# One feed-forward stage, three PSUM banks: seven-product units with a bank for each sum, later w_out words, logits without the clearing flag

## The chip, the cores and the metric

The kernel runs on 1 core of one Trainium2 chip. The metric is device time in microseconds (us) of one execution. The engines are named as in the profile: PE (matrix multiplies), DVE (vector), ACT (scalar), POOL (GpSimd), SP (which issues the DMAs).

## What is computed

```python
a = x @ w_a; b = x @ w_b              # x: 2304 x 512 (output of a banded attention), w: 512 x 1536
x = (a * b) @ w_out                   # feed-forward, w_out: 1536 x 512
logits = x @ phi                      # phi: 512 x 32 (8 experts x 4 slots)
d = softmax(logits, over tokens);  slot_input = d.T @ x
slot_out[e] = relu(slot_input[e] @ w1[e]) @ w2[e]
c = softmax(logits, over slots);   out = c @ slot_out
```

All of it is float32 to the reader of the output. The attention ahead of it is not touched by the change.

## The kernel before

After the attention x lies transposed in SBUF in five blocks of tokens (blocks 0 to 3 up to 512 wide, block 4 256). The 1536 columns of w_a and w_b are taken 128 at a time: f = 0 to 11. The product g = a*b is never multiplied by w_out: phi is folded into w_out first, M = w_out·phi (one 128x32 piece for each f), so that logits += M_f·g_f. Four products f = 0 to 3 of all blocks are made during the attention; the rest is the stage of this change.

**Units.** For blocks 0 and 1 and f = 4 to 11 the two halves of x and of the weights are taken as 2x2 matrices, and `unit(u, f, ...)` (u = f-4 = 0 to 7) makes a and b of both blocks by seven products in place of eight. Each product is six 128x512 matmuls (two k halves, three passes of float32 split in two words). There are three sums in PSUM, A, B and C, each in a bank of its own, which PE fills in this order: A (1st product), B (2nd), A (3rd), C (4th), A (5th), B (6th), A (7th). ACT copies A, B and C out between products, and C begins as an ACT copy of the first A. At the end DVE works out B += c2 (L2098), c1 *= B (L2099), POOL c3 += c4 (L2100), DVE c3 *= A (L2104), then DVE transposes c1 and c3 (L1305, L1307).

**PSUM.** Eight banks: a tag `m` with two banks, `m2` with one, `n` with one (the logits L of all blocks, a quarter of the bank each), `t` with four (transposes, M steps, slots). `UNIT_TAGS` gives A, B, C of even units the tags m, m, m2 and of odd units m2, m, m, so that each unit takes over banks of the one before it: an odd unit's B gets the bank in which A of the unit before was, an even unit's B that of the B before, and an even unit's C that of the A before.

**What runs between the products.** `gap(x)` puts small PE steps between products: logits of two units at every second one (`L`, L1325), and the M steps of w_out: four transposes (`wo`, L1337, copied by ACT at L1339), phi times it (`Mp`, L1344), a fold (`M`, L1352). A list of extras with clocks decides at which gap each comes; `extra(..., (("C", f), 2), ...)` asks that a `wo` comes two gaps after its words. `behind(x)` puts conversions on the other engines behind products: for the next unit the weights' raw 64-bit words are read (ACT `ra`, `rb` L921; DVE `wa`, `wb`: low word L927, whole word L939; DVE differences L1977; casts L1983; second words `la`, `lt` on DVE and `lu`, `lb` on POOL, L1989). `more()` steps through the same for one piece of w_out: rebias (ACT L921, behind ACT's copy of the third product), words (DVE L927 + L939, then the DMAs that store them and load the next raw piece, L903), and the M steps. The engines run their queues in the order in which the program issues.

**After the units** blocks 2, 3 and 4 are done with plain products (L1239), while softmax steps and slots of the block before run between: `soft` reads the logits (DVE L1373), `slots` takes four `t` banks. In `step_L` the first matmul of a block has the flag `start`, and for blocks 2 and up an `ensure(("S", ...))` puts `soft` of the block two before it ahead of that.

Of the kernel before, what the change touches and what calls it, by code (L numbers as in the profile page):

```python
# [14 lines left out]
ALU = mybir.AluOpType  # L15
# [168 lines left out]
def kernel(  # L184
# [1028 lines left out]
    close_psum(att_psum)  # L1213
    ffn_psum = open_psum(m2=1, n=1, t=4)
    post = ctx.enter_context(tc.tile_pool(name="post", bufs=1))
# [96 lines left out]
    def step_L(f, blk, src):  # L1312

        ensure(("M", f, "c", 0))
        if blk not in L_n:
            if blk >= 2:
                ensure(("S", blk - 2, 0))
            L_t[blk] = L_bank[:, blk % 4, :]  # L1320
            L_n[blk] = 0
        assert blk != 1 or 0 in L_n
        ps = L_t[blk]
        for j in range(len(TILES[blk])):
            nc.tensor.matmul(  # L1325
                ps[32 * j:32 * j + 32, :], lhsT=M[:, f, :], rhs=src[:, 128 * j:128 * j + 128],
                start=(L_n[blk] == 0 and blk != 1), stop=(L_n[blk] == NF - 1), skip_group_check=True,
            )
        L_n[blk] += 1
# [26 lines left out]
    def fin_steps(blk):  # L1356
# [80 lines left out]
        def slots(b):  # L1437


            def go():  # L1440
                if b == 0:
                    st["sl"] = [bank(PS["t"], "t", [128, UNIT], f"sl{blk}_{a}") for a in range(4)]
                for j in range(nj):
# [474 lines left out]
    def m_conv(f):  # L1918
# [11 lines left out]
        def fold():  # L1930
            tr, mm, fold = m_steps(f, box)
            x = M_ORDER.index(f)
            pair = M_ORDER[x - x % 2:x - x % 2 + 2]
            last = M_ORDER[x - 2:x - 1] if x > 1 else ()
            extra(0, ("M", f, "a"), [(("M", y, "b", 0), 0) for y in last] + [(("C", f), 2)], [(tr, 0, 0)])
            at["C", f] = clock[0]
            extra(0, ("M", f, "b"), [(("M", y, "a", 0), 1) for y in pair] + [(("M", y, "c", 0), 0) for y in last], [(mm, 0, 1)])
            extra(0, ("M", f, "c"), [(("M", f, "b", 0), 1)], [(fold, 0, 0)])
# [107 lines left out]

    UNIT_TAGS = (("m", "m", "m2"), ("m2", "m", "m"))

    def unit(u, f, gap, behind):

        tags = UNIT_TAGS[u % 2]
        b = {}
        d = half_t["tmp"]

        def prod(n, x, w, first):
            if first and n not in b:
                b[n] = bank(PS[tags["ABC".index(n)]], tags["ABC".index(n)], [128, 512], f"{n}{f}")
            wm, xm = pw(f, w), XS[x]
            todo = [(wm[:, wl, 128 * k:128 * k + 128], xm[:, xl, k, :]) for k in range(2) for wl, xl in PASSES]
            for i, (lhsT, rhs) in enumerate(todo):  # L2060
                nc.tensor.matmul(b[n], lhsT=lhsT, rhs=rhs, start=first and i == 0, stop=i == 5, skip_group_check=True)  # L2061
        V = nc.vector
        prod("A", "A11", "B11", True)
        b["B"] = bank(PS[tags[1]], tags[1], [128, 512], f"B{f}")
        gap(0)
        if u:
            b["C"] = bank(PS[tags[2]], tags[2], [128, 512], f"C{f}")
            nc.scalar.copy(b["C"], b["A"])
# [34 lines left out]
        prod("A", "A22", "T4", False)  # L2103
        V.tensor_tensor(c3, c3, b["A"], ALU.mult)  # L2104
        free_half(f"w{f}_U")
        gap(3)
        behind(6)
        step_T(f, 0, c1)
# [54 lines left out]
    with tc.manual_schedule():  # L2163
# [43 lines left out]
        def run_unit(n, f):  # L2207
# [27 lines left out]
            def behind(x):  # L2235
# [34 lines left out]
                elif x == 4:  # L2270
                    do("ht", "la")
                    more()
                elif x == 5:
                    do("lt")
                    more()
            unit(u, f, gap, behind)
            for blk in range(2):
                pend.append((0, f, blk))
            if f == NF - 1:
# [5 lines left out]
                let_ring_go()  # L2285
                m_n[0] = 2
            for name in ("xt2_0", "xt2_1", "gt2", "gt3"):
# [161 lines left out]
```

## Time and profile before

| | us |
|---|---|
| median of 3 runs | 523.38 |
| the three runs | 520.12, 523.38, 523.43 |
| the profiled execution | 521.03 |
| its span, first to last instruction | 519.0 |
| PE busy | 488.6 |
| DVE busy | 333.6 |
| ACT busy | 240.3 |
| the eight units, start to end on PE | 218.97 to 317.51 |

The span is what the trace covers; the execution's own time is 2 us longer. Times inside the trace are counted from the start of the span. The units fill about a fifth of it.

### The profile page before, as it was taken

What the parts mean: (1) busy time and instruction counts of PE and PEld (TensorE: products, weight loads), DVE (VectorE), ACT (ScalarE), POOL (GpSimd) and SP (SyncE); (2) the same over time, 40 slices, a digit from 0 to 9 for tenths busy, and PEclk for the clock granted to TensorE, in tenths of its full rate; (3) what the DMA queues carried; (4) which work ended last, traced back from release to release, by engine and by line L of the source; (5) the groups of instructions that cost most, each with busy time, mean ns of one, the idle gap of its engine ahead of it and who ended that gap; (6) DMA issues with size and microseconds to landing.
All of it is one profiled execution on the core that took longest, in us unless ns stands there. A gap on an engine that the chain in (4) does not pass through costs nothing.

```text
span 519.0 us, 15098 instructions
## 1 busy us (share of the span) xinstructions
PE 488.6 (94%) x6083; PEld 383.2 (74%) x6083; DVE 333.6 (64%) x1004; ACT 240.3 (46%) x692; POOL 132.7 (26%) x204
## 2 busy tenths in 40 slices
PE   7897899899989999989999999999999999999993
PEld 6775678778768899977767677767888988943552
DVE  5878786765764379879899976555466545342132
ACT  3775748576677234555556553331222332522122
POOL 6778777554530002012232231000000000101000
PEclk9998899999999999999999999999999999999998
DMA  9999977868791045596875435598628265699996
GB/s 176 214 177 171 186 123 130 130 121 116 105 291 43 3 125 169 185 301 192 271 266 188 149 123 180 204 352 309 255 83 278 87 239 187 265 319 341 349 359 236
DMA packets 147181, 103.81 MB, mean 200 GB/s; under 512 B 98344, under 2 KB 131368, under 8 KB 145960
## 3 DMA queue, kind: packets, MB, share of 16 engines
q1 hardware_dynamic: 145000, 102.32, 70.3%
q8 instruction: 48, 0.79, 0.7%
q10 hardware_dynamic: 2112, 0.52, 0.6%
q14 instruction: 21, 0.17, 0.1%
HBM read 87.10 MB, written 15.73 MB: 198 GB/s over the span
## 4 chain that ended last, share of the span: by engine, by line
PE 49%; DVE 4%; ACT 2%; DMA 2%; issue 1%; SPq 0%; DVEq 0%; ACTq 0%
PE b L1239 10%; PE a L1239 10%; PE A L2061 7%; PE B L2061 4%; PE sl L1447 3%; PE h L1695 3%; PE L L1325 3%; PE C L2061 2%; PE so L1681 2%; DMA ex<-in_moe_w_dram 2%; PE wo L1337 1%; DVE gn L1305 1%; PE T L1298 1%; PE Mp L1344 1%; PE stp L1518 1%
## 5 line engine op out<-in xcount | busy, mean ns | idle before, releaser
L587 ACT ACTIVATE P<-P,nm 128x128 f32<-128x128 f32 x128 | 49.9, 393 | 20.5 <-DVE nm L580 20.5
L970 PE MATMUL a<-xt,h_w 128*128 128x512 f32 x144 | 40.7, 413 | 1.4 <-DVE xt L696 1.1
L580 DVE CUSTOM_DVE_ANT_0 P<-s,lmask 128x128 f32<-128x128 f32 x128 | 28.8, 285 | 19.3 <-PE s L562 19.3
L1654 POOL TENSOR_TENSOR c<-CE,c 128x128 fp32r<-128x128 f32 (+1 forms) x5 | 2.9, 575 | 148.0 <-ACT c L1653 139.9
L970 PE MATMUL b<-xt,h_w 128*128 128x512 f32 x144 | 38.8, 405 | 0.0
L482 POOL TENSOR_SCALAR vw<-vw 32x896 f32<-32x896 f32 (+1 forms) x33 | 34.3, 1039 | 14.3 <-DMA vw<-in_v_l_dram 12.3
L1989 POOL TENSOR_TENSOR h_w_U<-scratch,h_w_U 128x512 fp32r<-128x512 f32 (+1 forms) x16 | 18.6, 1179 | 51.2 <-ACT h_w_U L1983 47.6
L970 PEld LDWEIGHTS a<-xt,h_w 128*128 128x128 f32 x144 | 25.9, 192 | 6.9 <-DVE xt L696 1.5
L970 PEld LDWEIGHTS b<-xt,h_w 128*128 128x128 f32 x144 | 25.5, 188 | 5.6 <-issue 1.1
L927 DVE TENSOR_SCALAR wr<-wr 128x512 int32<-128x512 int32 x36 | 23.5, 653 | 2.8 <-DMA wr<-in_moe_w_a_dram 2.5
L587 ACT ACTIVATION_READ_ACCUMULATOR P<-P,nm 128x1 f32 x128 | 24.3, 190 | 0.0
L2151 DVE TENSOR_TENSOR h_w<-h_w 128x512 fp32r<-128x512 f32 x24 | 16.3, 678 | 12.2 <-ACT h_w L2150 12.2
L1239 PE MATMUL a<-xt3a,h_w 128*128 128x384 f32 x120 | 22.9, 338 | 0.3 <-DVE gt L1244 0.3
L1239 PE MATMUL b<-xt3a,h_w 128*128 128x384 f32 x120 | 22.9, 339 | 0.0
L637 ACT COPY PT<-tp 128x512 f32<-128x512 f32 x32 | 18.6, 584 | 8.5 <-PE tp L632 8.2
L1262 ACT COPY gT<-a 128x512 f32<-128x512 f32 (+2 forms) x12 | 5.8, 485 | 34.0 <-PE L L1325 18.6
L1239 PEld LDWEIGHTS a<-xt3a,h_w 128*128 128x128 f32 x120 | 20.8, 188 | 0.9 <-DVE gt L1244 0.5
L1239 PEld LDWEIGHTS b<-xt3a,h_w 128*128 128x128 f32 x120 | 20.8, 188 | 0.9 <-issue 0.4
L632 PE MATMUL tp<-ident,P 128*128 128x128 f32 x128 | 20.2, 281 | 0.1
L562 PE MATMUL s<-kt,qt 64*32 64x128 f32 x1024 | 20.0, 291 | 0.1
L1239 PE MATMUL b<-xt3b,h_w 128*128 128x256 f32 x144 | 19.9, 288 | 0.0
L921 ACT ACTIVATE wr<-wr 128x512 f32<-128x512 f32 x28 | 19.2, 690 | 1.2 <-DMA wr<-in_moe_w_out_dram 0.9
(328 smaller groups left out, 1209.2 us busy)
## 6 DMA issues: line engine op xcount, KB each, us to landing
ex<-in_moe_w_dram SPq DMA_DIRECT2D x62, 512.0 KB, 6.5
wr<-in_moe_w_a_dram SPq DMA_DIRECT2D x12, 512.0 KB, 5.3
wr<-in_moe_w_b_dram SPq DMA_DIRECT2D x12, 512.0 KB, 5.3
wr<-in_moe_w_out_dram SPq DMA_DIRECT2D x12, 512.0 KB, 4.1
h_w<-wd SPq DMA_DIRECT2D x24, 256.0 KB, 3.7
wd<-scratch SPq DMA_DIRECT2D x16, 256.0 KB, 5.2
out_dram<-ob SPq DMA_DIRECT2D x7, 512.0 KB, 6.6
rawk<-in_k_l_dram SPq DMA_DIRECT2D x48, 64.0 KB, 3.5
```

Of the source, the lines that this page charges most:

```text
L482: nc.gpsimd.tensor_scalar(dst, src, 1.0, 1.0, ALU.mult, ALU.mult)
L562: nc.tensor.matmul(boxes[h]["s"][32 * (w % 4):32 * (w % 4) + 32, w // 4, :], lhsT=qt[rows, 32 * w:32 * w + 32], rhs=win_keys(kt, w)[rows], ...
L580: nc.vector.tensor_tensor_reduce(P[:, t, :], s[:, t, :], lmask[:, (t + 1) // 2, :], -scale, 3.0e38, ALU.add, ALU.min, nm[:, t:t + 1])
L587: nc.scalar.activation(P[:, t, :], P[:, t, :], AF.Exp, bias=nm[:, t:t + 1], scale=-1.0, accum_out=z_t[i][:, h, t:t + 1],)
L632: nc.tensor.transpose(box["ps"][:, t, :], P[:, t, :], ident)
L637: nc.scalar.copy(PT, box["ps"])
L921: nc.scalar.activation(hf, hf, AF.Prelu, scale=REBIAS, alpha=-TO_SIGN)
L927: nc.vector.tensor_scalar(v, v, 29, None, ALU.logical_shift_right)
L970: nc.tensor.matmul(box["ps"], lhsT=lhsT, rhs=rhs, start=(k + idx == 0), stop=(k == 3 and idx == 2))
L1239: nc.tensor.matmul(ps, lhsT=lhsT, rhs=rhs, start=(idx == 0), stop=(idx == 11))
L1989: eng.tensor_tensor(t[:, 1, c:], scratch(which)[:, c:], t[:, 0, c:].bitcast(F32), ALU.subtract)
L2061: nc.tensor.matmul(b[n], lhsT=lhsT, rhs=rhs, start=first and i == 0, stop=i == 5, skip_group_check=True)
```

## The change

It edits five things, all in the stage above.

1. The pools become m 2, m2 1, n 1, t 3 and a new tag `c` 1: A always takes `m` (its two banks in turn), B always `m2`, C always `c`. The slots of a block take three `t` banks and `c`.
2. DVE's last operation of a unit, c3 *= A, is issued after `gap(3)`. The M steps `words` of w_out come behind `lt` after the sixth product's sums, where they stood ahead of B += c2, the first of the sums; the step that enters the fold comes one later.
3. `wo` asks for four gaps after the words in place of two, which moves the M steps into other gaps and other units.
4. Logits of blocks 1, 2 and 3 have no `start` flag, only blocks 0 and 4 (block 4 shares a quarter with block 0). The `ensure` of `soft` stays for block 4 alone.
5. The counter by which plain products choose `m` or `m2` starts at 0 after the units, not 2.

```diff
@@ -1211,7 +1211,7 @@
     nc.sync.dma_start(out=phi_sb, in_=phi.rearrange("(k p) s -> p k s", p=128))
     att.release()
     close_psum(att_psum)
-    ffn_psum = open_psum(m2=1, n=1, t=4)
+    ffn_psum = open_psum(m2=1, n=1, t=3, c=1)
     post = ctx.enter_context(tc.tile_pool(name="post", bufs=1))
     pages.extend((post, f"q{n}") for n in range(6))
     build_late_consts(post)
@@ -1315,8 +1315,8 @@
 
         ensure(("M", f, "c", 0))
         if blk not in L_n:
-            if blk >= 2:
-                ensure(("S", blk - 2, 0))
+            if blk == 4:
+                ensure(("S", 2, 0))
             L_t[blk] = L_bank[:, blk % 4, :]
             L_n[blk] = 0
         assert blk != 1 or 0 in L_n
@@ -1324,7 +1324,7 @@
         for j in range(len(TILES[blk])):
             nc.tensor.matmul(
                 ps[32 * j:32 * j + 32, :], lhsT=M[:, f, :], rhs=src[:, 128 * j:128 * j + 128],
-                start=(L_n[blk] == 0 and blk != 1), stop=(L_n[blk] == NF - 1), skip_group_check=True,
+                start=(L_n[blk] == 0 and blk in (0, 4)), stop=(L_n[blk] == NF - 1), skip_group_check=True,
             )
         L_n[blk] += 1
 
@@ -1439,7 +1439,7 @@
 
             def go():
                 if b == 0:
-                    st["sl"] = [bank(PS["t"], "t", [128, UNIT], f"sl{blk}_{a}") for a in range(4)]
+                    st["sl"] = [bank(PS[t], t, [128, UNIT], f"sl{blk}_{a}") for a, t in enumerate("tttc")]
                 for j in range(nj):
                     for c0, g in g_unit(blk, 4 * j + b):
                         for a in range(4):
@@ -1932,7 +1932,7 @@
             x = M_ORDER.index(f)
             pair = M_ORDER[x - x % 2:x - x % 2 + 2]
             last = M_ORDER[x - 2:x - 1] if x > 1 else ()
-            extra(0, ("M", f, "a"), [(("M", y, "b", 0), 0) for y in last] + [(("C", f), 2)], [(tr, 0, 0)])
+            extra(0, ("M", f, "a"), [(("M", y, "b", 0), 0) for y in last] + [(("C", f), 4)], [(tr, 0, 0)])
             at["C", f] = clock[0]
             extra(0, ("M", f, "b"), [(("M", y, "a", 0), 1) for y in pair] + [(("M", y, "c", 0), 0) for y in last], [(mm, 0, 1)])
             extra(0, ("M", f, "c"), [(("M", f, "b", 0), 1)], [(fold, 0, 0)])
@@ -2044,27 +2044,25 @@
             return post.tile([128, n], F32, tag="gT", bufs=2, name="gT")
         return moe_p.tile([128, n], F32, tag="a", bufs=2, name="gT_a")
 
-    UNIT_TAGS = (("m", "m", "m2"), ("m2", "m", "m"))
+    UNIT_TAGS = dict(A="m", B="m2", C="c")
 
     def unit(u, f, gap, behind):
 
-        tags = UNIT_TAGS[u % 2]
         b = {}
         d = half_t["tmp"]
 
         def prod(n, x, w, first):
             if first and n not in b:
-                b[n] = bank(PS[tags["ABC".index(n)]], tags["ABC".index(n)], [128, 512], f"{n}{f}")
+                b[n] = bank(PS[UNIT_TAGS[n]], UNIT_TAGS[n], [128, 512], f"{n}{f}")
             wm, xm = pw(f, w), XS[x]
             todo = [(wm[:, wl, 128 * k:128 * k + 128], xm[:, xl, k, :]) for k in range(2) for wl, xl in PASSES]
             for i, (lhsT, rhs) in enumerate(todo):
                 nc.tensor.matmul(b[n], lhsT=lhsT, rhs=rhs, start=first and i == 0, stop=i == 5, skip_group_check=True)
         V = nc.vector
         prod("A", "A11", "B11", True)
-        b["B"] = bank(PS[tags[1]], tags[1], [128, 512], f"B{f}")
         gap(0)
         if u:
-            b["C"] = bank(PS[tags[2]], tags[2], [128, 512], f"C{f}")
+            b["C"] = bank(PS["c"], "c", [128, 512], f"C{f}")
             nc.scalar.copy(b["C"], b["A"])
         else:
             c1 = g_t[f, 0] = g_dest(512)
@@ -2101,9 +2099,9 @@
         free_half(f"w{f}_B")
         behind(5)
         prod("A", "A22", "T4", False)
-        V.tensor_tensor(c3, c3, b["A"], ALU.mult)
         free_half(f"w{f}_U")
         gap(3)
+        V.tensor_tensor(c3, c3, b["A"], ALU.mult)
         behind(6)
         step_T(f, 0, c1)
         step_T(f, 1, c3)
@@ -2269,9 +2267,10 @@
                     do("t12", "t34", "ha")
                 elif x == 4:
                     do("ht", "la")
-                    more()
                 elif x == 5:
                     do("lt")
+                    more()
+                elif x == 6:
                     more()
             unit(u, f, gap, behind)
             for blk in range(2):
@@ -2283,7 +2282,7 @@
                 w_t[f, 0] = w_t[f, "A"]
                 held[f"w{f}_0"] = held.pop(f"w{f}_A")
                 let_ring_go()
-                m_n[0] = 2
+                m_n[0] = 0
             for name in ("xt2_0", "xt2_1", "gt2", "gt3"):
                 if name in spilled and pages and u:
                     t = restore(name, F32R if name[0] == "x" else F32)
```

On DVE this is the end of unit 3 (B7, A7 are its sums; wr2_9 and cv are w_out's words, the L1989 rows are la and lt of unit 4), before:

```order
L1989 TENSOR_TENSOR h_w4_A_3578<-scratch_3523,h_w4_A_3578 128x512
L927 TENSOR_SCALAR wr2_9_4288<-wr2_9_4288 128x512
L939 SCALAR_TENSOR_TENSOR cv_4393<-wr2_9_4288 128x512
L2098 TENSOR_TENSOR B7_4324<-B7_4324,h_tmp_3526 128x512
L2099 TENSOR_TENSOR gT_a_4371<-gT_a_4371,B7_4324 128x512
L1989 TENSOR_TENSOR h_w4_A_3578<-scratch_3523,h_w4_A_3578 128x512
L2104 TENSOR_TENSOR gT_a_4388<-gT_a_4388,A7_4317 128x512
L1305 STREAM_TRANSPOSE gn0_0_3774<-gT_a_4371 128x5x32
```

and after, where c1 *= B and lt stand ahead of the two words (L927, L939), and c3 *= A alone behind them:

```order
L1989 TENSOR_TENSOR h_w4_A_3581<-scratch_3526,h_w4_A_3581 128x512
L2096 TENSOR_TENSOR B7_4312<-B7_4312,h_tmp_3529 128x512
L2097 TENSOR_TENSOR gT_a_4368<-gT_a_4368,B7_4312 128x512
L1989 TENSOR_TENSOR h_w4_A_3581<-scratch_3526,h_w4_A_3581 128x512
L927 TENSOR_SCALAR wr2_9_4281<-wr2_9_4281 128x512
L939 SCALAR_TENSOR_TENSOR cv_4406<-wr2_9_4281 128x512
L2104 TENSOR_TENSOR gT_a_4385<-gT_a_4385,A7_4300 128x512
L1305 STREAM_TRANSPOSE gn0_0_3777<-gT_a_4368 128x5x32
```

On PE these are the last product of unit 3 and the start of unit 4 up to its C (wo9, Mp8 and Mp9 are M steps; L the logits of the two units before; gt1 block 1's g of the first four f), before:

```order
L2061 MATMUL A7_4317<-xt1_1_1762,h_w4_U_3620 128x512 x6
L2061 MATMUL A8_4423<-xt0_0_596,h_w4_A_3578 128x512 x6
L1337 MATMUL wo9_4431<-ident_82,cv_4393 128x128 x4
L2061 MATMUL B8_4430<-S1_3517,h_w4_A_3578 128x512 x6
L2061 MATMUL A8_4423<-S2_3518,h_w4_A_3578 128x512 x6
L1325 MATMUL L_3497<-gT_4261,M_3491 32x128 x4
L1325 MATMUL L_3497<-gT_4274,M_3491 32x128 x4
L1325 MATMUL L_3497<-gT_a_4371,M_3491 32x128 x4
L1325 MATMUL L_3497<-gT_a_4388,M_3491 32x128 x4
L1344 MATMUL Mp8_4481<-woT_4330,phi_sb_88 32x128 x4
L1344 MATMUL Mp9_4488<-woT_4436,phi_sb_88 32x128 x4
L1325 MATMUL L_3497<-gt1_2017,M_3491 32x128 x8
```

and after, where B8 follows A8 with nothing between, wo9 stands behind the logits, and the two Mp are gone (they come in unit 5):

```order
L2060 MATMUL A7_4300<-xt1_1_1762,h_w4_U_3623 128x512 x6
L2060 MATMUL A8_4426<-xt0_0_596,h_w4_A_3581 128x512 x6
L2060 MATMUL B8_4438<-S1_3520,h_w4_A_3581 128x512 x6
L2060 MATMUL A8_4426<-S2_3521,h_w4_A_3581 128x512 x6
L1325 MATMUL L_3500<-gT_4250,M_3494 32x128 x4
L1325 MATMUL L_3500<-gT_4263,M_3494 32x128 x4
L1325 MATMUL L_3500<-gT_a_4368,M_3494 32x128 x4
L1325 MATMUL L_3500<-gT_a_4385,M_3494 32x128 x4
L1325 MATMUL L_3500<-gt1_2017,M_3494 32x128 x8
L1337 MATMUL wo9_4485<-ident_82,cv_4406 128x128 x4
L2060 MATMUL C8_4433<-xt0_1_913,h_w4_A_3581 128x512 x6
```

On DVE this is the place behind the units where `soft` of block 0 (lt0) stands beside the transposes of block 2's g (gt2), before:

```order
L1305 STREAM_TRANSPOSE gn2_2_4926<-gt2_4812 128x5x32
L1307 STREAM_TRANSPOSE gn2_0_4924<-gt2_4812 128x32
L1373 COPY lt0_4935<-L_3497 128x128
L1375 TENSOR_REDUCE mb0_4936<-lt0_4935 128x1
L1377 TENSOR_SCALAR nm0_4937<-mb0_4936 128x1
L1305 STREAM_TRANSPOSE gn2_0_4924<-gt2_4812 128x5x32
L1305 STREAM_TRANSPOSE gn2_1_4925<-gt2_4812 128x5x32
```

and after, where it stands two pieces of gt2 later, behind the last:

```order
L1305 STREAM_TRANSPOSE gn2_1_4928<-gt2_4795 128x5x32
L1305 STREAM_TRANSPOSE gn2_2_4929<-gt2_4795 128x5x32
L1307 STREAM_TRANSPOSE gn2_0_4927<-gt2_4795 128x32
L1373 COPY lt0_4962<-L_3500 128x128
L1375 TENSOR_REDUCE mb0_4963<-lt0_4962 128x1
L1377 TENSOR_SCALAR nm0_4964<-mb0_4963 128x1
L2149 TENSOR_TENSOR h_w4_U_3623<-h_w4_U_3623 128x512
```

## Rows read from the trace of the kernel before

**Rows 1.** Stretches of the span: busy us of each engine, granted clock, DMA share, GB/s.
```profile
219.10:316.00 96.90, 92.54 (x623) 72.36 (x622) 81.70 (x179) 54.64 (x116) 26.14 (x22) 1.00 0.63 206
345.00:380.00 35.00, 35.00 (x352) 27.81 (x353) 18.61 (x54) 7.76 (x15) 0.00 (x0) 1.00 0.72 261
455.00:519.00 64.00, 55.00 (x538) 26.84 (x535) 19.44 (x47) 14.76 (x41) 2.17 (x6) 0.96 1.00 325
```
**Rows 2.** Waits of PE in 219 to 345: us in total, times, longest.
```profile
PE B L2061 <- ACT woT L1339: 2.2, 3, 0.7
PE B L2061 <- DVE gT L2104: 1.9, 2, 1.7
PE L L1325 <- DVE lt L1373: 1.0, 1, 1.0
```
**Rows 3.** Timeline of PE in the units: start, us, tile; in brackets idle before.
```profile
233.90 1.62 PE L2061 MATMUL B<-S,h_w_A 128*128 128x512 f32 x6 [1.69 <-DVE gT L2104]
...
245.67 0.60 PE L1337 MATMUL wo<-ident,cv 128*128 128x128 f32 x4
246.02 1.63 PE L2061 MATMUL B<-S,h_w_A 128*128 128x512 f32 x6
...
266.16 1.55 PE L2061 MATMUL A<-xt,h_w_U 128*128 128x512 f32 x6
267.55 0.63 PE L2061 MATMUL A<-xt,h_w_A 128*128 128x512 f32 x2
...
270.88 1.70 PE L2061 MATMUL B<-S,h_w_A 128*128 128x512 f32 x6 [0.71 <-ACT woT L1339]
...
274.17 0.64 PE L1325 MATMUL L<-gT,M 128*32 128x128 f32 x16
...
284.83 1.62 PE L2061 MATMUL B<-S,h_w_A 128*128 128x512 f32 x6 [0.74 <-ACT woT L1339]
...
293.22 1.77 PE L2061 MATMUL A<-xt,h_w_A 128*128 128x512 f32 x6
...
299.57 0.65 PE L1325 MATMUL L<-gT,M 128*32 128x128 f32 x16
```
**Rows 4.** Timeline of DVE at the end of units 3, 4 and 7.
```profile
268.26 0.41 DVE L927 TENSOR_SCALAR wr<-wr 128x512 int32<-128x512 int32 x1
268.71 0.69 DVE L939 SCALAR_TENSOR_TENSOR cv<-wr 128x512 int32<-128x512 int32 x1
...
270.04 0.69 DVE L2099 TENSOR_TENSOR gT_a<-gT_a,B 128x512 f32<-128x512 f32 x1
...
279.90 1.52 DVE L927 TENSOR_SCALAR wr<-wr 128x512 int32<-128x512 int32 x1
...
316.39 0.70 DVE L2098 TENSOR_TENSOR B<-B,h_tmp 128x512 f32<-128x512 f32 x1 [5.85 <-PE B L2061]
```
**Rows 5.** Timeline of POOL at the end of units 4 and 7.
```profile
279.80 1.34 POOL L2100 TENSOR_TENSOR gT<-gT,h_tmp 128x512 f32<-128x512 f32 x1 [4.44 <-ACT M L1353]
...
315.62 1.29 POOL L2100 TENSOR_TENSOR gT_a<-gT_a,h_tmp 128x512 f32<-128x512 f32 x1 [3.34 <-ACT gT_a L2094]
```
**Rows 6.** Units 3, 4, 5 and 6, columns as in the first group.
```profile
257.00:267.50 10.50, 10.28 (x47) 8.29 (x46) 9.62 (x24) 6.91 (x13) 4.01 (x3) 1.00 0.86 274
267.50:282.10 14.60, 13.67 (x115) 10.07 (x115) 14.17 (x32) 7.60 (x17) 3.55 (x3) 1.00 0.61 201
282.10:293.20 11.10, 10.36 (x47) 8.31 (x46) 10.74 (x26) 7.08 (x13) 3.72 (x3) 1.00 0.52 159
293.20:307.50 14.30, 13.60 (x115) 10.06 (x114) 12.31 (x26) 7.01 (x16) 3.48 (x3) 1.00 0.49 169
```
**Rows 7.** Timeline of DVE behind the units: `soft` of block 0.
```profile
322.12 0.25 DVE L1373 COPY lt<-L 128x128 f32<-128x128 f32 x1
```
**Rows 8.** Timeline of PE among block 4's transposes T.
```profile
441.40 0.60 PE L1298 MATMUL T<-ident,a_two 128*128 128x128 f32 x4
```
**Rows 9.** Timeline of ACT at the same place: copies of T.
```profile
441.38 1.20 ACT L1299 COPY h_tmp<-T 128x256 f32<-128x256 f32 x4 [2.83 <-PE T L1298]
```
**Rows 10.** Issues of w_out's raw loads in 219 to 325: count, KB, median us to landing.
```profile
wr<-in_moe_w_out_dram SPq DMA_DIRECT2D x6, 512.0 KB, 4.0
```

## The prediction

> **What bounds the kernel now.** I first read the stretches of the span. In the units PE is busy 92.54 of 96.90 us and DVE 81.70 at a granted clock of 1.00, so PE sets the end and DVE stands close behind it; the DMA share is 0.63. In 455 to 519 PE is busy 55.00 of 64.00 us and the DMA share is 1.00: there the transfers set the end [rows 1]. Then PE's waits in the units: 2.2 us in three waits of B, which the view puts down to ACT's woT, and 1.9 in two put down to DVE's c3 *= A [rows 2]. The releaser has to be checked against which bank is whose. In unit 4, B8 has the bank of B7, which is free when c1 *= B has read it. That operation runs 270.04 + 0.69 = 270.73 [rows 4], and B8 starts at 270.88 [rows 3]. ACT's woT merely ended in the same tenth: the releaser is DVE. In odd units B has the bank of the A before, and c3 *= A is two operations later on DVE. So all five waits say one thing: the next unit's B waits for DVE's last sums, and ahead of those sums stand w_out's words, 0.41 + 0.69 us in unit 3 [rows 4].
>
> How much is lost there is more than the idle time, since the first products around the wait are stretched as well. An undisturbed product takes 1.39 us from start to start (266.16 to 267.55), a `wo` 0.35 (245.67 to 246.02) [rows 3]. Unit 4 needs 274.17 - 267.55 = 6.62 us for A, wo, B and A, where 3 x 1.39 + 0.35 = 4.52 would do: 2.10 lost. Unit 6 needs 299.57 - 293.22 = 6.35: 1.83 lost. Unit 1 idles 1.69, unit 5 idles 0.74 [rows 3], and the second of the c3 waits, in unit 3, is 1.9 - 1.7 = 0.2 [rows 2]. Sum: 2.10 + 1.83 + 1.69 + 0.74 + 0.2 = **6.6 us**.
>
> **The change part by part.**
>
> *Banks and the place of the words.* With B always in its own bank, B waits for c1 *= B of the unit before in all units, never for c3 *= A, and A alternates between two banks, so c3 *= A has a whole unit's time. On DVE c1 *= B and lt now come ahead of the words, that is 1.10 us earlier (0.41 + 0.69), and 2.2 earlier where the low word takes 1.52 [rows 4]. What the next B needs: the sixth product ends 1.39 before the unit does, then B += c2 and c1 *= B at 0.7 each [rows 4] end at about the end of the unit, and lt 0.7 after it, while the next B starts 1.39 after it and reads what lt wrote from its third matmul on. So there is a margin of about 1.4 us if DVE is on time, and the 6.6 go. Where DVE is late, some of it stays.
>
> Is DVE on time? In units 3 to 6 DVE is busy 9.62 + 14.17 + 10.74 + 12.31 = 46.84 us of 50.5 [rows 6]. PE's need there is 50.5 less the losses 0.2 + 2.10 + 0.74 + 1.83 = 4.87, so 45.6. By these sums DVE would be the bound by 1.2 us. But DVE's time holds a stretch that depends on the place: the low word took 0.41 in unit 3 and 1.52 in unit 4 [rows 4], where POOL's c3 += c4 ran from 279.80 for 1.34 [rows 5]. After the change c3 += c4 starts beside B += c2 and c1 *= B, and the words come later. Beside the same addition B += c2, which reads PSUM, isn't stretched: in unit 7 it takes 0.70 at 316.39 [rows 4], with POOL busy from 315.62 for 1.29 [rows 5]. If each of the four units is rid of one such stretch of 1.1, DVE needs 42.4 and keeps 3 us of air; if two are, 44.6, still under PE's 45.6. I take half a stretch, 0.5 us, as what stays of the loss in all, between 0 and one whole collision on the path (1.1). **Gain here 6.6 - 0.5 = 6.1**, bounds 5.5 and 6.6.
>
> The Trainium skill, in "SBUF — State Buffer", section "SBUF: two separate sides", says that DVE and GpSimd share a port pair as an exclusive lock, and that a DVE operation comes under it in a two-port mode or with two SBUF inputs. The 1.52 against 0.41 agrees. By that rule sums that read PSUM aren't held, all four stretches go and the residual is 0: the sum of this part would be 6.6.
>
> *M steps.* Their number stays: each `wo`, `Mp` and `M` costs PE what it did, and they go into other gaps of the same engine; price 0. The counter that starts at 0 only decides which free bank the first plain product takes: 0 too. The ACT copy woT moves from ahead of the copy C<-A to behind the copy of the third product, where it stands ahead of c1 and the rebias; ACT is busy 7.60 us of 14.60 in unit 4 [rows 6], so a copy of 0.6 finds cover. If the cover is gone, PE waits at most that copy in each unit; I hold this as part of the bound above, not as a term.
>
> *Words later, so w_out's DMAs later.* On SP the order of rows stays, but the store of the words and the next raw load are issued about 2 us later against PE. SP's queue behind them holds the next unit's raw weights, which are issued only with the words of that unit, so nobody is passed. The load has to land before ACT's rebias, ahead of c1's copy. In an odd unit C ends at about 4 x 1.39 + 3 x 0.35 (a wo and two Mp, each four matmuls, counted like the wo) = 6.6 us after the unit's start. The words end about 0.7 + 1.1 = 1.8 after it, by the reckoning above, so there are 4.8 us, and the loads land in 4.0 (median of six) [rows 10]. Price 0, with 0.8 us of air.
>
> *Logits without the flag.* The logits of block 2 waited 1.0 us for lt0, DVE's read of block 0's logits [rows 2]. This goes. But lt0 now stands behind all four pieces of gt2's transposes, two pieces later than its 322.12 [rows 7], about 1.8 us; the softmax copy behind it and the transposes DT then reach PE a little after the b product, where they were in time. I count 0.2 for that: **gain 0.8**, bounds 0 (all of it returns at DT) and 1.0. Block 3's `ensure` costs nothing now: PE is busy 35.00 of 35.00 us in 345 to 380 [rows 1].
>
> *Three t banks.* A use of `t` now waits for the copy of the use three before. Where uses come at a distance of products, that copy is long done. The one close row is block 4's: there four T, two matmuls each, come in a row, the last two of them in the row at 441.40, so the fourth starts at about 441.6; ACT's four copies begin at 441.38 and take 0.3 each, the first nearer to 0.4 [rows 8, 9]. The fourth T would wait for the end of the first copy, some 441.8: 0.2. Of the slots, the fourth bank (`c`) is free by then. **Cost 0.2**, bounds 0 and 0.5 (two more such places).
>
> The Trainium skill speaks against this part: "Perfetto Trace Analysis", section "Optimization Strategy" under "Identifying Performance Opportunities", reads repeated gaps as a sign of too few buffers. Here no row but this one is close; what the rule would make of the time is a rival below.
>
> Sum: 6.1 + 0.8 - 0.2 = **6.7 us**. Behind the units the pages that the late weight loads take are released by PE's own steps, so I carry the shift through to the tail. The profiled execution of 521.03 becomes 514.3; the median of the three runs, 523.38, lies 2.3 above it, which would give 516.7. I take 515.5 between the two.
>
> **The rivals.**
>
> *DVE is the bound* (the nearest). For: 46.84 busy against PE's need of 45.6 [rows 6]. It happens if POOL's addition, late itself, falls on differences and words as often as before, so that the stretch only moves. Then the four units take 46.84 + 0.9 of idle time (twice the 0.43 that unit 4 has: 14.60 - 14.17 [rows 6]) = 47.7 in place of 50.5, a gain of 2.8, with unit 1's 1.69, the seam's 0.8 and the 0.2: 5.1. That gives 515.9 on the profiled execution, 517.1 where I stand. With the bounds, 516 to 519.
>
> *The tail swallows it.* For: DMA share 1.00 over the last 64 us, PE busy 55.00 of them [rows 1]. If the transfers there were issued at times that don't depend on PE, they would end as before and the gain would turn into waits for weights: 0 to 2 us stay, 520 to 523. Against: a page must be released by PE before its load is issued.
>
> *Three t banks bind.* If every T and LT of block 4 waited 0.2 or more as in that row, 12 to 20 uses would cost 2.4 to 4, and the gain would be 3 to 4: 518 to 519.5. Against: the copies' starts in rows 9 follow the T at once.
>
> *w_out lands late* (slower). The rebias stands on ACT ahead of c1's copy, the cast ha and c3's copy, and the seventh product waits for c3's copy. The point: a landing over 4.8 us delays c1; PE notices when c3's copy comes later than the sixth product, another 1.39 less ACT's two copies of some 0.3 to 0.6. So it decides from about 5.6 us, and costs what is above it in each of six units. To end slower than before by 1% it must eat 6.7 + 5.2 us, 2 us a unit, a landing of 7.6: 527 to 529. The median of 4.0 [rows 10] speaks against it; that queues change with the load later speaks for a small chance.
>
> **How the numbers follow.** About 1% (5.2 us) is what a measurement of this kernel can tell from no change. Chances: forecast 0.60 (513.5 to 517.5), DVE the bound 0.20, t banks 0.06, tail 0.08, w_out late 0.06. Faster by over 1% (under 518.1): 0.58 of the forecast and half of the DVE rival, 0.68; slower 0.05; within 1% 0.27. The range goes down to 512, where all bounds hold and the launch is a fast one, and up to 520, past the DVE and t rivals.
>
> **What would show it.** In the trace after: no wait of B above 0.3 in units 1 to 7; units of 11.5 us on the mean (98.5 less 6.1, by eight); low words at 0.4 with c1 *= B ahead of them; POOL's c3 += c4 beside B += c2; L of block 2 straight behind gT_a; a short wait of DT instead; a T wait of some 0.2 in block 4. I am wrong if DVE shows no idle time in units 3 to 6 and PE still waits for lt or c1 *= B, if ACT's rebias waits for a DMA, or if the stretch from the end of the units to the end of the span grows by what the units lost.

## The result, and the profile after

| | before | after |
|---|---|---|
| median of the runs, us | 523.40 (4 runs) | 516.38 (4 runs, 515.25 to 517.32) |
| profiled execution, us | 521.03 | 517.32 |
| its span, us | 519.0 | 515.6 |
| the eight units on PE, us | 98.54 | 92.05 |

The ratio to the kernel before is 0.9886 with a 95% interval of [0.9845, 0.9928], some 6 us less; the two medians lie 7.0 apart. The same kernel once more, in five rounds, gave 515.49 and 0.9862 [0.9822, 0.9902]. The forecast was 515.5.

The units, from the first A to the first plain product, in the view of stretches (us, busy of PE, PEld, DVE, ACT, POOL, granted clock, DMA share, GB/s); first the kernel before, in the same cut:

```profile
218.97:317.51 98.54, 94.18 (x630) 73.70 (x629) 82.71 (x181) 54.70 (x116) 27.04 (x22) 1.00 0.63 203
```

and after:

```profile
220.89:312.94 92.05, 92.05 (x631) 74.00 (x630) 73.44 (x182) 54.29 (x117) 26.71 (x22) 1.00 0.67 218
...
255.00:302.00 47.00, 47.00 (x326) 37.87 (x325) 42.14 (x106) 27.92 (x59) 15.61 (x13) 1.00 0.71 228
256.16:302.06 45.90, 45.90 (x322) 36.95 (x321) 41.08 (x105) 27.92 (x59) 15.05 (x12) 1.00 0.70 224
```

PE is never idle in the units now. DVE does the same operations in 9.3 us less. The third row is units 3 to 6, from the first A of unit 3 to that of unit 7: 45.90 us on PE, where the prediction reckoned 45.6, with DVE busy 41.08, where it reckoned 42.4. (The second row, which experiment 4 goes by, begins 1.2 us ahead of unit 3.) PE's waits in 219 to 345 after, which answer to [rows 2], are down to one that has nothing to do with the change:

```profile
PE DT L1414 <- DVE acc L1460: 0.4, 1, 0.4
```

Timeline of PE after, unit 4 (to [rows 3]), start and us first:

```profile
267.43 1.52 PE L2060 MATMUL A<-xt,h_w_A 128*128 128x512 f32 x6
268.79 1.52 PE L2060 MATMUL B<-S,h_w_A 128*128 128x512 f32 x6
270.15 1.56 PE L2060 MATMUL A<-S,h_w_A 128*128 128x512 f32 x6
271.64 0.64 PE L1325 MATMUL L<-gT,M 128*32 128x128 f32 x16
```

A, B and A take 271.64 - 267.43 = 4.21 us, where A, wo, B and A took 6.62 (the wo, 0.35 us, now comes later in the unit). DVE at the same place (to [rows 4]):

```profile
266.26 0.70 DVE L2096 TENSOR_TENSOR B<-B,h_tmp 128x512 f32<-128x512 f32 x1 [0.46 <-PE B L2060]
266.99 0.69 DVE L2097 TENSOR_TENSOR gT_a<-gT_a,B 128x512 f32<-128x512 f32 x1
267.60 0.68 DVE L1989 TENSOR_TENSOR h_w_A<-scratch,h_w_A 128x512 fp32r<-128x512 f32 x1
268.20 0.42 DVE L927 TENSOR_SCALAR wr<-wr 128x512 int32<-128x512 int32 x1
268.65 0.69 DVE L939 SCALAR_TENSOR_TENSOR cv<-wr 128x512 int32<-128x512 int32 x1
269.26 0.68 DVE L2104 TENSOR_TENSOR gT_a<-gT_a,A 128x512 f32<-128x512 f32 x1
```

c1 *= B ends at 267.68, 1.1 us ahead of the next B at 268.79. DVE even waits 0.46 for PE ahead of B += c2. Where DVE's 9.3 us went is read from the groups by line, of before (busy, mean ns):

```profile
L927 DVE TENSOR_SCALAR wr<-wr 128x512 int32<-128x512 int32 x21 | 15.1, 721 | 0.3 <-DMA wr<-in_moe_w_b_dram 0.3
L1977 DVE TENSOR_TENSOR scratch<-scratch 128x256 f32<-128x256 f32 x28 | 12.7, 494 | 0.3
L939 DVE SCALAR_TENSOR_TENSOR cv<-wr 128x512 int32<-128x512 int32 x7 | 6.8, 978 | 0.2
```

and after:

```profile
L927 DVE TENSOR_SCALAR wr<-wr 128x512 int32<-128x512 int32 x21 | 9.5, 453 | 0.1
L1977 DVE TENSOR_TENSOR scratch<-scratch 128x256 f32<-128x256 f32 x28 | 10.5, 415 | 0.3
L939 DVE SCALAR_TENSOR_TENSOR cv<-wr 128x512 int32<-128x512 int32 x7 | 4.8, 692 | 0.4
```

The three groups give back 5.6 + 2.2 + 2.0 = 9.8 us; all else together takes some 0.5 more. Not all of it was lost beside the same POOL operation. The low words of L927 are seven of w_out and fourteen of the raw a and b weights. Two of w_out's took 1.52 beside POOL's addition c3 += c4, so 2.2 of the 5.6 are theirs; with the differences and the whole words (L939) that makes 6.4 us beside the addition. The other 3.4 are low words of a and b, which stand at the start of a unit beside POOL's second words (lu, lb), in unit 4 before:

```profile
273.15 2.21 POOL L1989 TENSOR_TENSOR h_w_U<-scratch,h_w_U 128x512 fp32r<-128x512 f32 x2 [6.03 <-ACT h_w_U L1983]
273.42 1.33 DVE L927 TENSOR_SCALAR wr<-wr 128x512 int32<-128x512 int32 x1
```

and after, where this low word begins 1.2 us behind POOL's pair and not 0.3:

```profile
270.23 2.20 POOL L1989 TENSOR_TENSOR h_w_U<-scratch,h_w_U 128x512 fp32r<-128x512 f32 x2 [3.29 <-ACT h_w_U L1983]
271.44 0.41 DVE L927 TENSOR_SCALAR wr<-wr 128x512 int32<-128x512 int32 x1
```

Six of them were stretched before (0.87 to 1.33 us), one is after (1.15).

Between fixed points of PE's timeline, us:

| stretch | before | after | change |
|---|---|---|---|
| units | 98.54 | 92.05 | -6.49 |
| to block 3's first product | 58.74 | 58.48 | -0.26 |
| to block 4's first slots | 80.77 | 81.05 | +0.28 |
| to the sums of the second expert product (sor) | 37.32 | 37.32 | 0 |
| to the end of the span | 24.66 | 25.81 | +1.15 |
| ahead of the units | 218.97 | 220.89 | +1.92 |

The first three are the change's, -6.47 us together. What lies ahead of the units does the same work, and its length differs from execution to execution: 218.97 to 222.01 in the thirteen traces of this study, both ends of it in kernels with DVE's order of before. The last stretch is tested below.

### The profile page after: what moved, and what is told of

The parts are those of the page before. It is cut to its first block, busy times and chain, and to the rows that moved or that the text cites. A ratio compares the mean times of both kernels' runs of the same rounds, so it can differ in the third digit from the quotient of the medians.

```text
span 515.6 us, 15097 instructions
## 1 busy us (share of the span) xinstructions
PE 487.6 (95%) x6083; PEld 383.5 (74%) x6083; DVE 330.0 (64%) x1004; ACT 239.4 (46%) x692; POOL 132.3 (26%) x204
## 4 chain that ended last, share of the span: by engine, by line
PE 52%; DVE 2%; DMA 2%; ACT 1%; issue 1%; DVEq 0%; ACTq 0%
PE a L1239 10%; PE b L1239 10%; PE A L2060 8%; PE B L2060 4%; PE sl L1447 3%; PE h L1695 3%; PE L L1325 2%; PE so L1681 2%; PE C L2060 2%; DMA ex<-in_moe_w_dram 2%; PE wo L1337 1%; DVE gn L1305 1%; PE Mp L1344 1%; PE T L1298 1%; PE stp L1518 1%; PE sl L1469 1%
## 5 line engine op out<-in xcount | busy, mean ns | idle before, releaser
L1989 POOL TENSOR_TENSOR h_w_U<-scratch,h_w_U 128x512 fp32r<-128x512 f32 (+1 forms) x16 | 17.8, 1130 | 41.7 <-ACT h_w_U L1983 41.7
L927 DVE TENSOR_SCALAR wr<-wr 128x512 int32<-128x512 int32 x36 | 22.0, 611 | 0.1
L562 PEld LDWEIGHTS s<-kt,qt 64*32 64x32 f32 x1024 | 15.3, 108 | 6.2 <-issue 3.7
```

The lines of the kernel that those rows point to most:

```text
L562: nc.tensor.matmul(boxes[h]["s"][32 * (w % 4):32 * (w % 4) + 32, w // 4, :], lhsT=qt[rows, 32 * w:32 * w + 32], rhs=win_keys(kt, w)[rows], ...
L927: nc.vector.tensor_scalar(v, v, 29, None, ALU.logical_shift_right)
L1989: eng.tensor_tensor(t[:, 1, c:], scratch(which)[:, c:], t[:, 0, c:].bitcast(F32), ALU.subtract)
```

## The experiments

Each quotes what was expected; "units" is the stretch of the eight units on PE, which took 98.54 us before and 92.05 after the change.

**1. Banks alone, order alone.** The kernel before with the pools, tags and slots of the change only (label e1_banks), and with its order only (e2_words):

```diff
-    UNIT_TAGS = (("m", "m", "m2"), ("m2", "m", "m"))          # e1_banks, with the pools and slots
+    UNIT_TAGS = dict(A="m", B="m2", C="c")
```

```diff
                     do("ht", "la")                            # e2_words, with c3 *= A behind gap(3) and wo at 4
-                    more()
                 elif x == 5:
                     do("lt")
+                    more()
+                elif x == 6:
                     more()
```

> Only the banks are changed (A, B and C in their own tags, three t banks, slots t t t c); w_out's words stay ahead of the sums, the M steps and the flag stay as before. The stretch of the eight units on PE was 98.5 us before and is 92.05 after the whole change. Theory (banks and order of DVE's sums are both needed): units 1, 3 and 5 now wait for c1 *= B in place of c3 *= A, so their 1.7 + 0.2 + 0.7 us go, but units 4 and 6 waited for c1 *= B already and keep theirs; units 95.5 to 96.5, time 1.5 to 3 us under the kernel before. Rival 1 (banks alone carry it): units 92 to 93, time as the changed kernel, about 6 us under before. Rival 2 (the order of the words alone carries it): units 98, no gain.

> Only the order is changed: words behind lt, c3 *= A last, M steps four gaps later; the old banks (B of odd units in the bank of the A before, C of even units likewise) and four t banks stay. Theory (both needed): B of units 1, 3 and 5 waits for c3 *= A, which now stands behind the words as well, about 1.1 us each, and even units' copy C<-A waits for it too, some 0.4 each; units 95.5 to 97, time 1 to 3 us under before, PE's waits put down to c3 *= A. Rival 2 (order alone carries it): units 92 to 93, 6 us under before. Rival 1 (banks alone): units 98 or more, no gain.

Measured: e1 519.34 us, 0.993 [0.9896, 0.9965], units 96.68; e2 520.7 us, 0.9952 [0.9922, 0.9982], units 97.39. Of PE's waits, one in unit 4 of e1:

```profile
270.24 1.71 PE L2060 MATMUL B<-S,h_w_A 128*128 128x512 f32 x6 [0.76 <-ACT woT L1339]
```

and in units 3 and 4 of e2:

```profile
258.83 1.63 PE L2061 MATMUL B<-S,h_w_A 128*128 128x512 f32 x6 [1.10 <-DVE gT L2106]
...
272.05 1.66 PE L2061 MATMUL A<-S,h_w_A 128*128 128x512 f32 x6 [0.35 <-ACT C L2068]
```

Both were a little dearer than expected (units 95.5 to 96.5 and 95.5 to 97), but the places are the expected ones. With banks alone, units 4 and 6 keep the wait for c1 *= B behind the words; with order alone, units 3 and 5 wait 1.10 for c3 *= A (unit 1 0.27) and even units 0.35 for the copy C<-A behind it. Alone they save 1.9 and 1.2 us, together 6.5: neither rival holds, each part takes away one of two operations that B waited for.

The row of e1 names ACT's woT, which ends at the same 270.09 as c1 *= B does there. That B doesn't wait for woT shows in unit 2 before: B starts at 246.02, while the wo that woT copies runs from 245.67 for 0.60 [rows 3].

**2. M steps back at their old distance.**

```diff
-            extra(0, ("M", f, "a"), [...] + [(("C", f), 4)], [(tr, 0, 0)])
+            extra(0, ("M", f, "a"), [...] + [(("C", f), 2)], [(tr, 0, 0)])
```

> The changed kernel with the M steps back at their old distance (wo two gaps after the words, so again between a unit's first product and its B, and Mp and M in even units again). Banks, the order of DVE's sums and the flag stay changed. Theory: the words now end at 268.65 + 0.69 = 269.3 where B starts at 268.8, so a wo ahead of B waits for them, 0.5 to 0.8 us in each of units 1 to 6, and c1 *= B isn't the releaser any more; units 94.5 to 97, PE's waits put down to the words (L939). Rival (the place of the M steps is of no weight, price 0 as the prediction has it): units 92 to 92.5.

One execution of 524.32 us; units 99.75, longer than before the change and than the 94.5 to 97 expected. A row of its PE timeline:

```profile
273.52 0.66 PE L1337 MATMUL wo<-ident,cv 128*128 128x128 f32 x4 [1.79 <-DVE cv L939]
```

The wo waits 5.2 us in five places for the words, 0.54 in three of them and 1.8 in units 4 and 6, where A itself waits 0.4 for la: DVE as a whole is late there, on which the expectation didn't reckon. So the one number 2 -> 4 is no detail: with the words late, the old place of wo between A and B costs 7.7 us over the units.

**3. w_out later still.** Words behind the transposes of c1 and c3:

```diff
         step_T(f, 1, c3)
+        behind(7)
...
                     do("lt")
+                elif x == 7:
                     more()
-                elif x == 6:
                     more()
```

> The changed kernel with w_out's words moved further back, behind the transposes of c1 and c3, so that they end some 2.5 us later against PE, and the store and the next raw load with them. DVE's order ahead of B is untouched. Theory (the slower rival's mechanism is real and its point is near: ACT's rebias already idles 0.4 to 0.6 us for this load in odd units after the change): the rebias is 2.5 us later in odd units, c1's and c3's copies behind it, and the seventh product waits some 1 to 1.6 us in units 1, 3 and 5, up to 0.5 in 2, 4 and 6; units 95 to 98, time 3 to 6 us over the changed kernel. Alternative (air of 0.8 us and more behind it, as the prediction counted): units under 93.5.

Measured 524.18 us, 1.0043 [1.0012, 1.0075] to the kernel before, 7.8 over the changed kernel where 3 to 6 were expected; units 101.24 where 95 to 98 were. ACT after the change and here, at the rebias of an odd unit; after the change:

```profile
262.88 0.67 ACT L921 ACTIVATE wr<-wr 128x512 f32<-128x512 f32 x1 [0.63 <-DMA wr<-in_moe_w_out_dram]
263.45 0.57 ACT L2084 COPY gT_a<-C 128x512 f32<-128x512 f32 x1
264.43 0.59 ACT L2092 COPY gT_a<-A 128x512 f32<-128x512 f32 x1
```

and with the words later, ACT and then PE's waits:

```profile
266.92 0.67 ACT L921 ACTIVATE wr<-wr 128x512 f32<-128x512 f32 x1 [3.21 <-DMA wr<-in_moe_w_out_dram]
```

```profile
PE A L2060 <- ACT gT L2092: 4.6, 2, 2.5
PE A L2060 <- ACT gT_a L2092: 3.2, 2, 1.7
```

The slower rival's mechanism is real: the seventh product waits for c3's copy, up to 2.5 us, in units 2 to 5, most in the even ones, where at most 0.5 was expected. Its point is near. After the change the rebias already waits 0.63 us for the load, and c3's copy ends at 265.02, 1.04 us ahead of the seventh product at 266.06. That 1 us is all the air there is in unit 3.

**4. More work for DVE.**

```diff
-                    do("ht", "la")
+                    do("ht", "la", "la", "la")
```

> The changed kernel with la done three times in place of once in each unit (same result), that is 1.4 us more of DVE ahead of B += c2. After the change DVE is busy 42.1 of 47.0 us in units 3 to 6, and idles 0.5 to 0.9 us ahead of B += c2. If DVE's work is the next bound (theory): 42.1 + 4 x 1.4 = 47.7, over PE's 47.0; DVE has no idle time left, PE waits for lt or c1 *= B, units 93 to 95.5. If DVE still has air of a unit's order (margin of B 1.4 us as counted): no waits, units 92.0 to 92.4.

One execution of 524.78 us; units 100.72, against 93 to 95.5 expected. DVE:

```profile
281.73 3.11 DVE L1989 TENSOR_TENSOR h_w_A<-scratch,h_w_A 128x512 fp32r<-128x512 f32 x3
284.75 0.69 DVE L2096 TENSOR_TENSOR B<-B,h_tmp 128x512 f32<-128x512 f32 x1
```

with POOL busy beside it:

```profile
282.17 1.40 POOL L2098 TENSOR_TENSOR gT<-gT,h_tmp 128x512 f32<-128x512 f32 x1 [5.22 <-ACT gT L2092]
```

The direction was right and the size not: three la take 3.11 where 3 x 0.69 = 2.1 were counted. Once DVE is late, POOL's addition no longer falls beside B += c2 and the idle time ahead of it, but on la, which it stretches, and a unit's time becomes DVE's (B += c2 follows B += c2 after 284.75 - 271.99 = 12.76 us). With two more la a unit the rival "DVE is the bound" is the case; at how much less it begins no run shows.

**5. POOL's addition given to DVE**, in the kernel before:

```diff
-        nc.gpsimd.tensor_tensor(c3, c3, c4, ALU.add)
+        V.tensor_tensor(c3, c3, c4, ALU.add)
```

> The kernel before the change with one operation of each unit, c3 += c4, done by DVE in place of POOL. Over the units DVE was busy 82.7 us before and 73.4 after the change for the same operations. Theory (POOL's addition stretches DVE's operations that run beside it): DVE gets 8 x 0.69 = 5.5 us of work more and is rid of the stretch, so it is busy 79 to 82 us, and the low words of w_out take 0.4 us in every unit; units 96.5 to 98.5. Rival (the stretch has another cause, DMAs or the place in the unit): DVE 87 to 89 us, low words of 1.5 us as before, units 100 or more.

One execution of 523.75 us; units 97.84, DVE busy:

```profile
222.01:319.85 97.84, 93.81 (x631) 73.94 (x629) 80.72 (x188) 54.49 (x116) 16.11 (x14) 1.00 0.64 205
```

80.72 with 5.5 us of work more than before's 82.71; the low words of w_out take 0.42 in every unit, its whole words 0.69 and the differences 1.5 for four. For these three the stretch is POOL's addition, not the place. The low words of a and b stay stretched, since POOL still makes second words beside them; in unit 4:

```profile
275.52 1.31 DVE L927 TENSOR_SCALAR wr<-wr 128x512 int32<-128x512 int32 x1
```

So the expectation was right about the addition, and the 9.3 us that the change gave back aren't the addition's alone.

**6. Less work ahead of the tail.** The changed kernel without the seventh product of units 1 to 7:

```diff
-        prod("A", "A22", "T4", False)
+        if u == 0:
+            prod("A", "A22", "T4", False)
```

> The changed kernel without the seventh product of units 1 to 7 (their second half of blocks lacks one term): PE is rid of 7 x 1.38 = 9.7 us in the units, nothing of the DMAs or of the work behind them is left out. Theory (what PE saves ahead of the tail is carried through to the end): units about 82.5 us, if DVE with some 74 us of work keeps up, and the time 9 to 9.7 us under the changed kernel, the stretch from the units' end to the last instruction as long as after the change (202.6) within 1 us. Rival (the tail, with its transfers at full rate, swallows it): that stretch grows by 3 us or more. If DVE doesn't keep up, the units stay above 84 us with waits for DVE, and the gain is that much less.

Measured 510.65 us, 0.9756 [0.9729, 0.9783]; units 86.81, not 82.5: DVE is busy 71.72 of them and PE waits for la and c1 *= B again. From the units' end to the end of the span it takes 202.9 us, against 202.7 after the change (201.5 in experiment 7). The last stretch (sor to the end) is 24.72, as before the change, though it begins 8.9 us earlier in its trace than in that of before (at 485.5 against 494.3). What PE saves arrives at the end. (The 1.3 us more between units and block 3 are DVE's lateness, seen in a wait of DT.)

**7. The changed kernel once more.**

> The changed kernel once more, unedited. In its first profile the last stretch, from the sums of the second expert product (sor) to the end of the span, took 25.81 us, against 24.66 before and 24.3 to 24.8 in six variants whose code there is the same. Theory (the extra 1.1 us is one execution's, not the change's): 24.3 to 24.9 here; units 92.05 within 0.05, since nothing there waits. Rival (the changed kernel's earlier arrival costs 1.1 us at the weight loads): 25.5 to 26.

Units 92.05, last stretch 201.52 - 176.80 = 24.72 (both from the units' end). The 1.15 us of the first profile didn't come back, so I take them as that execution's.

**8. The seam.** Three orders of block 2's logits L, block 0's `soft` and gt2's transposes T: soft behind the first L (e7_seam); all L, soft, T (e11_seam2, with the bank c for three T of block 4); all L, soft, T two products later (e12_seam3, with the same bank):

```diff
+        if blk in (2, 3) and L_n[blk] == 1:                                # e7_seam, in step_L
+            ensure(("S", blk - 2, 0))
```

```diff
+            if blk == 2 and f == 0:                                        # e11_seam2, ahead of T
+                for x in range(F0):
+                    step_L(x, blk, gt0[blk][:, x, :])
+                ensure(("S", 0, 0))
...
+            t = "c" if f in (3, 4, 8) else "t"                             # in step_T, block 4
```

```diff
+                extra(0, ("GT", f, blk), [(("G", f, blk, 0), 1 + f // 2)], [(turn, 0, 0)])   # e12_seam3
```

> The changed kernel, but the reading of block 0's logits (soft) is issued right behind the first logits of block 2, so that it stands between the second and third piece of gt2's transposes on DVE, as before the change, while the logits of block 2 still don't wait for it. The b product of block 2's second pair (the one behind the first slots) started 14.04 us after the units' end before and 13.71 after the change. If the small gain there is due to the place of lt0 (theory): DT at once behind the b product, and this start at 13.0 to 13.2, so 0.5 us under the changed kernel in the trace. If it is not (something else bounds the stretch): 13.6 to 13.8. The time itself can hardly tell: 0 to 0.6 us.

> The changed kernel with two mends. At the seam all four logits of block 2 are issued first, then soft of block 0, then the transposes of gt2, so lt0 waits for neither and nobody waits for it. And in block 4 every fourth transpose in a row (f = 3, 4 and 8) takes the bank c in place of a t bank. Theory: the start of the b product behind the first slots goes from 13.71 to 12.8 to 13.0 us after the units' end; from block 3's first product to block 4's slots (81.05 us after the change, 80.77 before) it takes 80.75 to 80.85. Together 0.9 to 1.2 us under the changed kernel in the trace, time 514.5 to 516. If the seam's loss has another cause: 13.5 to 13.8.

> As the run before (all logits of block 2 first, then soft of block 0, a c bank for every fourth transpose of block 4), but gt2's four pieces of transposes are put off: two pieces behind the sums of the next product, two behind the one after, so that DVE makes the second words of the weights (h_w_U, L2151 before) ahead of them. From the units' end to block 3's first product it took 58.74 us before, 58.48 after the change, 58.74 in the run with soft alone moved ahead of the transposes, where PE waited 0.7 us for h_w_U. Theory (the seam is held by DVE's queue, 3.8 us of transposes in it, wherever soft stands): 57.3 to 58.0 and no wait for h_w_U. If something else holds it: 58.4 or more. With 0.24 us for block 4, 0.7 to 1.4 us under the changed kernel in the trace, time 514 to 515.8.

| | time, us (ratio, interval) | units' end to block 3 | to block 4's slots |
|---|---|---|---|
| after | 516.38 | 58.48 | 81.05 |
| e7_seam | 514.9 (0.9836 [0.98, 0.9873]) | 58.59 | 81.02 |
| e11_seam2 | 515.28 (0.9864 [0.9823, 0.9904]) | 58.74 | 80.81 |
| e12_seam3 | 515.3 (0.9869 [0.9845, 0.9893]) | 58.19 | 80.81 |

The measurement can't tell the times apart; the traces can. e7 and e11 missed: the start of the b product came at 13.87 and 14.02 us, not 12.8 to 13.2. In e7 the later L wait 0.8 for lt0, though the logits of block 2 have no flag there: that they're issued behind lt0 is enough for the wait. With lt0 early, the a product behind it takes 3.01 us and the slots 1.92, as before the change (3.27 and 2.22 after it), but the wait takes what they give. In e11 it is the other way round: lt0 waits for all four L, with DVE's queue behind it,

```profile
317.74 0.29 DVE L1374 COPY lt<-L 128x128 f32<-128x128 f32 x1 [1.67 <-PE L L1326]
```

so that h_w_U comes late, and PE waits on:

```profile
322.29 2.57 PE L1239 MATMUL a<-xt,h_w_U 128*128 128x512 f32 x10 [0.66 <-DVE h_w_U L2155]
```

Putting T off (e12) takes that wait of PE away and gives 0.29 us, of 0.5 to 1.2 expected; lt0's 1.67 and a wait of 0.2 for the next h_w_U remain. The c bank gives back 0.24 of 0.28 us in block 4.

## Why the prediction was right

*The units* (6.1 forecast, 6.49 measured). The reading of PE's waits held: the sum of lost time by rows was 6.6. Experiment 1 shows both halves of the step, bank and order, at their places. What I kept as a residual of 0.5 didn't appear: no operation ahead of the next B is stretched beside POOL's addition any more. DVE's 41.1 in units 3 to 6 lies near the 42.4 of the step, but not by the step's reckoning. It took one stretch of 1.1 beside the addition from each of the four units; there were three (in unit 6 none), and about as much again, 3.1 us, lay on low words of a and b beside POOL's second words, which the step hadn't seen. Experiments 4 and 5 show that the stretches of w_out's words, differences and la are the addition's, and that they come back as soon as DVE is late. So the rival with the next chance was no weak one: with two more la a unit it is the case. The lock of the Trainium skill in "SBUF — State Buffer", section "SBUF: two separate sides", agrees with the pairs seen here: two-input differences, words and la are stretched by 1.0 to 1.2 us beside the addition, B += c2 from PSUM isn't (0.70).

*M steps at price 0.* True of the change as it stands, wrong as a reason: they didn't merely go into other gaps of the same engine. With the words behind lt, wo at the old place costs 7.7 us (experiment 2).

*w_out's load at price 0, with 0.8 us of air.* The time agrees, but the 0.8 of air wasn't there: the load lands just as C ends. In unit 3 the words end at 258.06, 1.9 us after the unit's start (1.8 reckoned), and the rebias that waits for the load starts 4.8 us later, at 262.88; the loads land in 4.4 us (median of six) after their issue, against 4.0 before. The sign that I had named for being wrong, a rebias that waits for a DMA (0.63), did appear, and it cost nothing: the copies behind the rebias have 1 us left. Experiment 3 shows where it would decide.

*Logits without the flag* (0.8 forecast, 0.26 measured; e1 and e2, which keep the flag and the `ensure`, take 58.77 and 58.74 to block 3, so the 0.26 comes with this part or with the counter of plain products, which wasn't run apart). This is the step that was mis-sized. I counted lt0's lateness as 0.2 at DT, where it is 0.28, and named nobody else behind it. ACT after, at the seam:

```profile
319.91 0.72 ACT L1391 ACTIVATE dT<-lt,nm 128x512 f32<-128x512 f32 x1 [3.07 <-DVE nm L1377]
320.54 0.19 ACT L1391 ACTIVATION_READ_ACCUMULATOR dT<-lt,nm 128x1 f32 x1
320.63 0.60 ACT L2148 CAST h_w_U<-h_w_U 128x512 fp32r<-128x512 f32 x1
```

and DVE behind it:

```profile
321.26 0.69 DVE L2149 TENSOR_TENSOR h_w_U<-h_w_U 128x512 fp32r<-128x512 f32 x1 [1.39 <-ACT h_w_U L2148]
```

The cast of the next weights is queued on ACT behind the exponential that waits for lt0. It starts 7.69 us after the units' end (320.63 - 312.94), where it started 6.13 after it before. The a product of those weights then takes 3.27 us in place of 3.01 and the slots 2.22 in place of 1.92. Of the 0.89 us that the a product was early, 0.33 is left when b follows and 0.26 at block 3. In e7, with lt0 and the cast early, both are short again; in e11, where h_w_U is late by another way, both are long. So their stretch goes with h_w_U's lateness; by which operand the slots are held no row shows. That DVE's queue of T holds the seam is shown by experiment 8 only in part: e12 moved 0.29 us by it. And to be issued behind lt0 is by itself enough to make the L wait (e7); what the flag adds to that isn't shown.

*Three t banks* (0.2 forecast, 0.28 measured). The one place was the right one; PE after, against 0.60 in [rows 8]:

```profile
436.60 0.85 PE L1298 MATMUL T<-ident,a_two 128*128 128x128 f32 x4
```

It comes with the pools alone too (81.03 in e1_banks), and goes with a c bank there.

*The tail.* Carried through, as forecast: the table of stretches, experiments 6 and 7. The rival that the transfers swallow it is out.

*The sum.* 6.1 + 0.8 - 0.2 = 6.7 against 6.49 + 0.26 - 0.28 = 6.47 in the trace. That it comes within 0.2 is partly luck: the units gave 0.4 more than forecast and the logits 0.5 less.

## What to carry to other kernels

When a product waits at the start of each unit, find all the operations that its PSUM bank and its operands wait for, and move all of them ahead of the work that nobody waits for: half the move here was worth 1 to 2 us, the whole 6.5. Whoever puts an operation later in one queue has to look at each consumer of what it makes, PE's small steps and the next load included, and at what stands behind that consumer on its own engine. When two engines disturb each other, their time is no fixed sum: busy time before the change made DVE look like the bound, and 9 of its 82.7 us in the units were stretches beside POOL.

## What was not expected of the hardware

The size of the collision: the same DVE operations took 82.7 or 73.4 us according to what POOL did beside them, with eight additions of 1.3 to 1.85 us and seven pairs of second words of 2.0 to 2.6. A low word took 0.42 alone and up to 1.52 beside the addition. After the change the addition is in units 3 and 5 the one that is longer: 1.84 where la of 0.69 began in the same moment, 1.29 in even units 2 to 6. The return is as steep: two more la in seven units, which follow one another at 0.60 us (so 8.4 us in all), made DVE busy 86.6 us in the units in place of 73.4 and cost PE 8.7.
